# Cross attention and a squared-ReLU MLP: the second layer of the slot-read rows as seven block products, with a split bias and new order keys

## Chip, cores and metric

The kernel runs on one core of one Trainium2 chip. The metric is the device time of that core in microseconds, from the first to the last instruction of one execution. Kernels were timed in turns with the kernel before on the same chip.

## The reference

There are two parts. Eight batches of eight heads (S = 512 rows, Ns = 32 state slots, D = 64) read across from x to the state, and from the state to x. The two results, 512 + 32 rows in each batch, go through one two-layer MLP (512 to 2048 to 512).

```python
scores = scale * x @ state^T;   a  = softmax(scores);    xread = a  @ state   # 512 rows a batch
scores2 = scale * state @ x^T;  a2 = softmax(scores2);   sread = a2 @ x       #  32 rows a batch
rows = concatenate([xread, sread])        # (8 * 544) rows of 8 heads * 64 = 512
h = rows @ w_in                           # 512 -> 2048
g = s * relu(h) ** 2 + b
out = g @ w_out                           # 2048 -> 512, float32
```

The 8 x 32 = 256 rows of `sread` are called the slot-read rows, `sr` in the names of the tiles. They are worked on together, at the end. The constant `b` adds the same vector to every row, `b` times the column sums of `w_out`.

## The kernel before

All work is put into one list of operations. Each has an engine, an estimated duration, a key, what it needs, what it makes and the buffers that it holds. `Plan.order` then simulates the engines and takes, for each engine that is free, the ready operation with the lowest key. The program is written out in that order, so a change of a key or of a duration in the list moves instructions everywhere. These are its lines that the change touches:

```python
class Plan:
    def __init__(self, caps, hop=0.2, look=0.4): ...
    # ... in order():
        def settle(i):
            since[i] = max([ops[i][8]] + [ready[n] for n in ops[i][3]])
    # ...
                    k = ops[i][1] + 20.0 * max(0.0, t)
                    if e == "PE" and ops[i][7] and mode:     # a tiled matmul after a tiled one
                        k -= 4.0
    # ...
                for m in makes:
                    ready[m] = done + self.hop
```

Batches 1 to 7 already compute their second layer as seven block products (in the manner of Strassen and Winograd) in place of eight. The activations are cut into 2 x 2 blocks of rows and hidden columns, `w_out` into 2 x 2 blocks. `pair_sums` makes sums of activation blocks (`pd`), `weight_sum` sums of weight blocks (`u`). The products gather in two PSUM banks `ob`:

```python
    STEPS = [            # bank, activation block, weight block, first, last
        (0, 4, 4, True, False), (1, 6, 6, True, True), (0, 2, 1, False, False), (1, 1, 0, True, False),
        (0, 0, 2, False, False), (1, 3, 7, False, True), (0, 7, 3, False, True),
    ]
    TAKE = {0: ("c11", 0), 2: ("c12", 1), 3: ("c22", 1), 6: ("c21", 0)}     # evict to a new tile, plus bias
    GIVE = {1: "c11", 4: "c22", 5: "c12"}                                   # evict on top of that tile
    PUT = {1: ("c11", 0, 0), 4: ("c22", 1, 1), 5: ("c12", 0, 1), 6: ("c21", 1, 0)}      # store
    # ...
    for b in range(1, B):
        for n in range(7):
            # ... 8 x step_mm (two matmuls 128x256 each), step_out on VectorE, step_put
```

The slot-read rows do it the plain way, in two tiles of 128 rows. The first tile takes 16 matmuls of 512 columns, the second 2 x 16 of 256, so that its first half can be stored early:

```python
    def sr_dst(rr):
        return out_BSn[4 * rr : 4 * rr + 4, S:ST, :]        # 4 batches x 32 rows x 512
    # ...
    for part in range(4):
        add(PEt(0.864), NKF * (B + 1) + part, rows_mm("sr", 0, 4 * part, 4 * part + 4), ...)
    add(DV(0.66), -50, rows_out("sr", 0), ...)
    add(("SP", 0.6), 0, rows_put("sr", 0, sr_dst(0)), ...)                       # 256 KB
    # ... last_mm: the second tile, 256 columns at a time
    for i in range(2):
        for part in range(4):
            add(PEt(0.436), NKF * (B + 1) + 5 + 4 * i + part, last_mm(i, part), ...)
        add(DV(0.4), -50, last_out(i), ...)
        add(("SP", 0.6), 0, last_put(i), ...)                                    # 128 KB each
```

The bias vector is summed over the hidden rows by tiled matmuls, copied, and spread to all partitions by a matmul with a matrix of 1/Ns, in float32:

```python
    def bias_copy(e):
        OSB["wsum"] = opool.tile([P, DM], FP32, name="wsum", tag="osb")
        copy_on(e, OSB["wsum"], OSB["wsum_ps"])

    def bias_spread(e):
        OSB["bias_ps"] = att_ps([P, DM], FP32, "bias_ps")
        mm(OSB["bias_ps"], ones32, OSB["wsum"])
```

The softmax here doesn't subtract the row's maximum and nothing guards it: scores larger than these inputs give would overflow.

## Time and profile before

| kernel before | |
|---|---|
| time | 219.19 us, 218.91 to 219.51 in four runs |
| span of the profiled execution | 217.1 us |
| first matmul of an MLP first layer (`h`) | 13.87 us |
| bias spread | starts at 37.48 us |
| first matmul of the slot-read rows' second layer | 201.87 us |
| last matmul starts | 209.50 us |
| from there to the end ("the tail") | 7.64 us |

The first line of the page gives the busy time of each engine, its share of the span and its instructions. The second is the chain of work that ended last, by engine.

```profile
PE 205.8 (95%) x1967; PEld 132.0 (61%) x1967; DVE 164.6 (76%) x389; ACT 134.5 (62%) x294; POOL 37.4 (17%) x60
...
PE 90%; ACT 2%; DVE 2%; DMA 2%; SPq 0%; issue 0%
```

TensorE (PE) is the limit: it is busy 95% of the span and makes up 90% of the chain. The table by windows shows where that holds. Its columns are the window in us, then busy time and instructions of PE, weight loads (PEld), VectorE (DVE), ScalarE (ACT) and GpSimd (POOL), the granted clock, the mean busy share of the 16 DMA engines (it can read above 1), and GB/s.

```profile
core 0: us, PE busy (x) PEld busy (x) DVE busy (x) ACT busy (x) POOL busy (x), PEclk, DMA share, GB/s
...
50.00:75.00 25.00, 25.00 (x296) 15.71 (x294) 21.66 (x49) 16.60 (x37) 6.28 (x10) 1.00 1.11 149
...
150.00:175.00 25.00, 25.00 (x265) 17.68 (x263) 21.52 (x49) 14.49 (x26) 3.37 (x5) 1.00 0.20 63
...
207.00:208.25 1.25, 1.25 (x14) 1.13 (x12) 0.00 (x0) 0.00 (x0) 0.00 (x0) 1.00 0.63 215
209.75:214.75 5.00, 0.02 (x1) 0.00 (x0) 0.48 (x1) 0.00 (x0) 0.00 (x0) 1.00 0.26 87
```

In mid-kernel PE has no idle time at all, so there only the number and length of its instructions count.

PE's idle time is at the start. Each line of the waits view gives engine and line, what was waited for, total us, number of waits and the longest. Of the tiles, `xn` is x as loaded, `xT` its transpose, `T` the scores, `E` their exponentials, `D` the sums of these, and `M` the state times `w_in`:

```profile
PE xTps L197 <- ACT xn L298: 1.5, 2, 1.2
PE o L197 <- DVE warm L212: 1.2, 1, 1.2
PE h L197 <- ACT g L760: 0.6, 2, 0.4
PE Mps L197 <- DVE M L300: 0.3, 1, 0.3
PE Mps L197 <- ACT M L298: 0.2, 1, 0.2
PE T L197 <- DVE xT L300: 0.2, 1, 0.2
```

The timeline gives start, duration, engine, line, operation and count. Two cuts of it matter, the bias spread and the end:

```profile
37.48 1.02 PE L197 MATMUL bias_ps<-wsum,ones 128*128 128x512 f32 x2
38.34 1.06 PE L197 MATMUL xTps<-ident,xn 128*128 128x128 f16 x16
...
205.11 4.66 PE L197 MATMUL o<-wo,g_sr 128*128 128x512 f16 x36
...
209.81 0.48 DVE L1079 SCALAR_TENSOR_TENSOR osb_last<-o,s_bc,bias_bc 128x256 f32<-128x256 f32 x1 [0.39 <-PE o L197]
...
206.96 0.66 SPq L912 DMA_DIRECT2D out_dram<-osb_sr  x1
209.45 1.41 SPq L1088 DMA_DIRECT2D out_dram<-osb_last  x2
```

Read the starts, not the durations: matmuls overlap, and the next start shows what one took of the stream. The float32 spread is two records and takes 38.34 - 37.48 = 0.86 us. After the last eviction at 209.81 comes only a store. Its issue begins at 210.32 and SyncE (SPq), which waits for all stores before the program may end, is released by it at 216.18, 5.9 us later. The waits of SyncE's queue at the end are these:

```profile
SPq L1134 <- DMA out_dram<-osb_last: 2.6, 2, 1.3
```

### The profile page before, as it was taken

The numbers are of one execution on the slowest core, as the hardware profiler recorded it, in microseconds if no ns is written. First come the engines' busy times: TensorE is split into PE (matmuls) and PEld (weight loads), VectorE is DVE, ScalarE is ACT, GpSimd is POOL, SyncE is SP. The second block draws the span as 40 slices with busy tenths as digits, with TensorE's granted clock in tenths as the row PEclk, the third lists the DMA queues.
The fourth block names the chain that finished last, engine by engine and source line by source line (L and its number), as shares of the span: only waits on it lengthen the run. The fifth ranks groups of instructions, "written<-read, shape, count | busy, mean of one in ns | idle before, by whom it ended". The sixth has DMA issues, their size and how long they took to land.

```text
span 217.1 us, 4922 instructions
## 1 busy us (share of the span) xinstructions
PE 205.8 (95%) x1967; PEld 132.0 (61%) x1967; DVE 164.6 (76%) x389; ACT 134.5 (62%) x294; POOL 37.4 (17%) x60
## 2 busy tenths in 40 slices
PE   5998999999999999999999999999999999999960
PEld 1452334434477776677667666776677777888550
DVE  1268899999888889789978897889888888654320
ACT  4479998587585469747874797479645545332100
POOL 4833100040134251012101210121012102100000
PEclk9999999999999999999999999999999999999997
DMA  6999999999599999413531205122212102111131
GB/s 194 179 199 205 207 202 194 176 147 209 55 161 207 154 194 125 113 51 103 121 76 48 101 32 75 49 73 84 50 48 97 49 8 85 63 48 47 53 85 60
DMA packets 41282, 24.04 MB, mean 111 GB/s; under 512 B 25772, under 2 KB 39340, under 8 KB 41260
## 3 DMA queue, kind: packets, MB, share of 16 engines
q0 software_dynamic: 13840, 15.21, 36.6%
q1 hardware_dynamic: 26860, 8.40, 24.6%
q8 instruction: 15, 0.25, 0.5%
q10 hardware_dynamic: 560, 0.13, 0.3%
q14 instruction: 7, 0.06, 0.1%
HBM read 17.37 MB, written 8.91 MB: 121 GB/s over the span
## 4 chain that ended last, share of the span: by engine, by line
PE 90%; ACT 2%; DVE 2%; DMA 2%; SPq 0%; issue 0%
PE o L197 52%; PE h L197 24%; PE Mps L197 4%; PE h_sr L197 3%; PE D L197 2%; DMA xf<-in_x_dram 2%; ACT g L760 1%; PE V L197 1%; PE xTps L197 1%; PE T L197 1%; DVE g L766 1%; DVE xT L300 1%; PE wsum_ps L197 0%; ACT M L298 0%; PE bias_ps L197 0%; ACT xn L298 0%
## 5 line engine op out<-in xcount | busy, mean ns | idle before, releaser
L760 ACT ACTIVATE g<-h 128x512 f16<-128x512 f32 x125 | 73.3, 604 | 42.8 <-PE h L197 40.9
L197 PE MATMUL h<-a,M 128*128 128x512 f16 x256 | 73.7, 379 | 0.6 <-ACT g L760 0.6
L766 DVE TENSOR_TENSOR g<-g 128x512 f16<-128x512 f16 x128 | 52.9, 420 | 7.0 <-ACT g L760 6.4
L197 PEld LDWEIGHTS <-pd 128*128 128x128 f16 x448 | 43.0, 98 | 19.0 <-issue 2.8
L197 PEld LDWEIGHTS <-g 128*128 128x128 f16 x400 | 38.5, 98 | 22.1 <-issue 1.8
L197 PE MATMUL o<-u,pd 128*128 128x256 f16 x336 | 51.8, 273 | 0.0
L197 PE MATMUL o<-wo,g 128*128 128x256 f16 (+1 forms) x288 | 51.6, 296 | 0.0
L1002 POOL DMA_DIRECT2D out_dram<-c x24 | 16.3, 678 | 104.5 <-DVE c L994 101.5
L298 ACT CAST M<-Mps 128x512 f16<-128x512 f32 x52 | 29.4, 608 | 4.0 <-PE Mps L197 4.0
L197 PEld LDWEIGHTS <-M 128*128 128x128 f16 x256 | 24.2, 98 | 12.5 <-issue 3.9
L994 DVE SCALAR_TENSOR_TENSOR c<-o,s_bc,bias_bc 128x512 f32<-128x512 f32 x28 | 21.0, 751 | 12.7 <-PE o L197 12.7
L197 PE MATMUL o<-u,g 128*128 128x256 f16 x112 | 21.4, 273 | 0.0
L197 PE MATMUL o<-wo,pd 128*128 128x256 f16 x112 | 21.4, 273 | 0.0
L994 DVE SCALAR_TENSOR_TENSOR c<-o,s_bc,c 128x512 f32<-128x512 f32 x21 | 15.8, 750 | 6.7 <-PE o L197 6.6
L778 DVE TENSOR_TENSOR pd<-g 128x1024 f16<-128x1024 f16 x28 | 19.2, 685 | 0.2
L760 ACT ACTIVATE g_sr<-h_sr 128x256 f16<-128x256 f32 x16 | 6.1, 384 | 13.1 <-PE h_sr L197 13.0
L527 ACT ACTIVATE E<-T 128x256 f16<-128x256 f32 x32 | 11.8, 385 | 1.3 <-PE T L197 1.2
L787 DVE TENSOR_TENSOR pd<-g,pd 128x512 f16<-128x512 f16 x28 | 11.7, 419 | 0.0
L789 DVE TENSOR_TENSOR pd<-g,pd 128x512 f16<-128x512 f16 x28 | 11.7, 420 | 0.1
L374 POOL DMA_DIRECT2D xn<-in_x_dram x13 | 10.4, 813 | 7.6 <-DMA wi<-in_moe_w_in_dram 3.2
L546 ACT ACTIVATE D<-D 128x512 f32<-128x512 f32 x16 | 8.7, 582 | 2.5 <-PE D L197 2.4
L197 PE MATMUL h_sr<-srdT,wi 128*128 128x256 f16 x64 | 9.6, 273 | 0.0
(63 smaller groups left out, 157.5 us busy)
## 6 DMA issues: line engine op xcount, KB each, us to landing
out_dram<-c POOLq DMA_DIRECT2D x24, 256.0 KB, 2.5
xn<-in_x_dram POOLq DMA_DIRECT2D x5, 512.0 KB, 22.0
wi<-in_moe_w_in_dram POOLq DMA_DIRECT2D x4, 512.0 KB, 13.5
wo<-in_moe_w_out_dram POOLq DMA_DIRECT2D x4, 512.0 KB, 18.8
xf<-in_x_dram SPq DMA_DIRECT2D x4, 256.0 KB, 3.4
out_dram<-osb POOLq DMA_DIRECT2D x4, 256.0 KB, 5.7
xn<-in_x_dram POOLq DMA_DIRECT2D x8, 128.0 KB, 4.9
out_dram<-c SPq DMA_DIRECT2D x4, 256.0 KB, 2.5
```

What stands on the lines that cost most here:

```text
L197: return nc.tensor.matmul(out, lhsT, rhs, start=start, stop=stop, tile_position=tp, is_transpose=is_transpose, skip_group_check=True,)
L298: nc.scalar.copy(dst, src)
L374: nc.gpsimd.dma_start(out=xn[b][:, h0:h1].rearrange("p h c d -> p h (c d)"), in_=x[b, h0:h1].rearrange("h (q c) d -> q h (c d)", q=P),)
L527: nc.scalar.activation(a["E"][g][:, 256 * m : 256 * m + 256], a["T"][m][:, g, :], AF.Exp, scale=scale, accum_out=a["rs"][:, g, m : m + 1],)
L546: nc.scalar.activation(A[b][f"D{g}"], A[b][f"D{g}"], AF.Ln)
L760: nc.scalar.activation(g_of(name, f), OSB["h", name, f], AF.Relu)
L766: ENG[e].tensor_mul(g_of(name, f), g_of(name, f), g_of(name, f))
L778: nc.vector.tensor_tensor(pd[:, :, 0:2], g4[:, :, 1:2, :].to_broadcast((P, 2, 2, hS)), g4[:, :, 0:4:3, :], ALU.subtract,)
L787: nc.vector.tensor_tensor(pd[:, :, 2], g4[:, :, 3], pd[:, :, 0], ALU.subtract)
L789: nc.vector.tensor_tensor(pd[:, :, 3], g4[:, :, 2], pd[:, :, 2], ALU.subtract)
L994: nc.vector.scalar_tensor_tensor(t, src, s_bc, add, ALU.mult, ALU.add)
L1002: ENG[e].dma_start(dst[:, rows:SCH:2, hD * h : hD * h + hD], SN[b, name])
```

## The change

Three things are changed. The slot-read rows get the same seven products as the batches (seven times eight matmuls of 256 columns in place of 16 of 512 and 32 of 256). These take turns in two PSUM banks of their own, taken from the pool `att` that the attention no longer needs then. VectorE gets 12 pair sums more, 7 evictions in place of 3, and there are four stores of 128 KB. The float32 matmul of the bias becomes two in fp16: the sum rounded to fp16 and the remainder. And the list scheduler is changed: a delay between operations (`hop`) counts only between different engines, a tiled operation that stands alone on TensorE gets a penalty (`solo`), and all keys are set anew, with the estimated landing times of the first loads 0.2 us lower.

```diff
-    def __init__(self, caps, hop=0.2, look=0.4):
+    def __init__(self, caps, hop=0.2, look=0.4, solo=0.0):
...
-            since[i] = max([ops[i][8]] + [ready[n] for n in ops[i][3]])
+            own = set(ops[i][0])
+            since[i] = max(
+                [ops[i][8]]
+                + [ready[n] + (0.0 if own == {made_on.get(n)} else self.hop) for n in ops[i][3]]
+            )
...
+                    if alone and ops[i][7]:
+                        k += self.solo
...
     K = dict(
-        h1=4.3, hs=0.6, M0=-5.6, M1=0.9, T1=0.9, x2=24.4, T2=23.7, D2=25.5, M2=24.1, V0=27.6, V1=20.5, u=12.2,
-        us=5.1, pd1=12.5, o0=9.6, o2=23.0, w=26.2, r=0.7, T=-14.8, D=3.1, Mb=5.5, V=8.6, S=3.6, S0=0.1, E=-4.5,
-        L=-4.6, a4=-4.7, Mc=4.3, pd=3.5, sp=-1.7,
+        h1=4.4, hs=0.6, M0=-5.6, M1=0.9, T1=0.0, x2=24.6, T2=23.7, D2=27.2, M2=35.3, V0=27.7, V1=21.3, u=12.3,
+        us=5.1, pd1=12.5, o0=13.1, o2=23.0, w=26.2, r=0.5, T=-9.8, D=3.1, Mb=6.4, V=8.6, S=3.6, S0=0.1, E=-0.5,
+        L=-6.2, a4=-4.7, Mc=1.5, pd=13.4, solo=2.0, hsr=-4.1, Ssr=0.0,
     )
...
     def bias_copy(e):
-        OSB["wsum"] = opool.tile([P, DM], FP32, name="wsum", tag="osb")
-        copy_on(e, OSB["wsum"], OSB["wsum_ps"])
+        OSB["wsum"] = opool.tile([P, 2, DM], FP16, name="wsum", tag="osb")
+        nc.vector.tensor_copy(OSB["wsum"][:, 0], OSB["wsum_ps"])
+        nc.vector.tensor_tensor(OSB["wsum"][:, 1], OSB["wsum_ps"], OSB["wsum"][:, 0], ALU.subtract)
 
     def bias_spread(e):
         OSB["bias_ps"] = att_ps([P, DM], FP32, "bias_ps")
-        mm(OSB["bias_ps"], ones32, OSB["wsum"])
+        for k in range(2):
+            mm(OSB["bias_ps"], ones_p, OSB["wsum"][:, k], start=(k == 0), stop=(k == 1))
...
+    def bank_of(b, n):
+        if b != "sr":
+            return ob[(STEPS[n][0] + b) % 2]
+        if ("bank", STEPS[n][0]) not in OSB:
+            OSB["bank", STEPS[n][0]] = att_ps([P, DM], FP32, f"osr_{STEPS[n][0]}")
+        return OSB["bank", STEPS[n][0]]
...
             name, rows, h = PUT[n]
+            if b == "sr":
+                dst = out_BSn[4 * rows : 4 * rows + 4, S:ST, hD * h : hD * h + hD]
+                ENG[e].dma_start(dst, SN[b, name][:, 0])
+                return
...
-    for b in range(1, B):
+    for b in [*range(1, B), "sr"]:
+        nb = B if b == "sr" else b
         for n in range(7):
...
-    for part in range(4):
-        add(
-            PEt(0.864), NKF * (B + 1) + part, rows_mm("sr", 0, 4 * part, 4 * part + 4),
...  (the plain second layer of the slot-read rows, last_mm, last_out and last_put go)
```

More of the change, by code (lines that the diff above doesn't have):

```diff
@@ L14 @@
 class Plan:
-    def __init__(self, caps, hop=0.2, look=0.4):
-        self.caps, self.hop, self.look = caps, hop, look
+    def __init__(self, caps, hop=0.2, look=0.4, solo=0.0):
+        self.caps, self.hop, self.look, self.solo = caps, hop, look, solo
         self.ops, self.pool_of, self.users = [], {}, {}
@@ L31, in order @@
         waits, count, cand = {}, {}, {e: set() for e in ("PE", "ACT", "DVE", "POOL", "SP")}
-        since = {}
+        since, made_on = {}, {}
         def settle(i):
-            since[i] = max([ops[i][8]] + [ready[n] for n in ops[i][3]])
+            own = set(ops[i][0])
[3 more added lines that the diff above has]
+            )
             for e in ops[i][0]:
@@ L72, in order @@
                 best = None
+                alone = False
+                if e == "PE" and not mode:
+                    near = [i for i in cand[e] if ops[i][7] and since[i] <= now + 0.3 and soon(i) <= now + 0.3]
+                    alone = len(near) < 2 or sum(len([b for b in ops[i][5] if self.pool_of[b] == "att"]) for i in near[:2]) > (
+                        self.caps["att"] - sum(x not in freed for x in allocs["att"])
+                    )
                 look = self.look if e in ("ACT", "DVE") else 0.06
@@ L123, in order @@
                 for m in makes:
-                    ready[m] = done + self.hop
+                    ready[m], made_on[m] = done, (e if land is None else None)
                 for m in makes:
@@ L240 @@
     nc.vector.memset(ones16, 1.0)
-    ones32 = konst.tile([P, P], FP32, name="ones32")
-    nc.vector.memset(ones32, 1.0 / Ns)
+    ones_p = konst.tile([P, P], FP16, name="ones_p")
+    nc.vector.memset(ones_p, 1.0 / Ns)
     s_bc = konst.tile([P, 1], FP32, name="s_bc")
@@ L306 @@
             "u": 4, "osb": 6, "q": 2, "rs": 3,
-        }
+        },
+        solo=K["solo"],
     )
@@ L389 @@
     nc.gpsimd.tensor_copy(gate, ident16[:, 0:2])
-    seq = [("wi", 0), ("x", 1), ("wi", 1), ("stf1",), ("wo", 0), ("wi", 2), ("wo", 1), ("wi", 3)]
-    seq += [("wo", 2), ("wo", 3), ("x", 2), ("sb",), ("x", 3), ("x", 4), ("x", 5)]
+    SEQ = "wi0 x1 wi1 stf1 wo0 wi2 wo1 wi3 wo2 wo3 x2 sb x3 x4 x5"
+    seq = [(t,) if t in ("stf1", "sb") else (t[:-1], int(t[-1])) for t in SEQ.split()]
     for n, it in enumerate(seq):
@@ L768, in square, with half_of @@
         return fn
+    def half_of(b):
+        return B * Ns // 2 if b == "sr" else S // 2
     def blocks(b, j):
@@ L776, in fn @@
             if n == 0:
-                pd = PD[b, j] = ppool.tile([P, 2, 4, hS], FP16, name=f"pd_{b}_{j}", tag="pd")
+                t = half_of(b)
+                pd = PD[b, j] = ppool.tile([P, 2, 4, t], FP16, name=f"pd_{b}_{j}", tag="pd")
                 nc.vector.tensor_tensor(
                     pd[:, :, 0:2],
-                    g4[:, :, 1:2, :].to_broadcast((P, 2, 2, hS)),
+                    g4[:, :, 1:2, :].to_broadcast((P, 2, 2, t)),
                     g4[:, :, 0:4:3, :],
@@ L878 @@
     add(PEt(0.9), K["w"], bias_sum, [("wo", q) for q in range(4)], ["wsum_ps"], [("att", "wsum_ps")], tiled=True)
-    add(DV(0.6), 20, bias_copy, ["wsum_ps"], ["wsum"], [("att", "wsum_ps"), ("osb", "wsum")])
-    add(PEt(0.88), 24, bias_spread, ["wsum"], ["bias_ps"], [("att", "bias_ps"), ("osb", "wsum")])
+    add(DV(1.25), 20, bias_copy, ["wsum_ps"], ["wsum"], [("att", "wsum_ps"), ("osb", "wsum")])
+    add(PEt(0.44), 24, bias_spread, ["wsum"], ["bias_ps"], [("att", "bias_ps"), ("osb", "wsum")])
     add(DV(0.6), 20, bias_out, ["bias_ps", ("b",)], ["bias"], [("att", "bias_ps")])
@@ L885, in x_dst @@
         return out_BSn[b, 0:S].rearrange("(q c) n -> c q n", c=SCH)[chunk_of(rr)]
-    def sr_dst(rr):
-        return out_BSn[4 * rr : 4 * rr + 4, S:ST, :]
     def rows_mm(name, rr, f0, f1):
@@ L964 @@
     ]
+    def bank_of(b, n):
[4 more added lines that the diff above has]
+        return OSB["bank", STEPS[n][0]]
     def step_mm(b, n, i):
         def fn(e):
-            bank, xa, xw, first, last = STEPS[n]
-            for r in range(2):
+            _, xa, xw, first, last = STEPS[n]
+            for r in range(half_of(b) // P):
                 mm(
-                    ob[(bank + b) % 2][:, hD * r : hD * r + hD],
+                    bank_of(b, n)[:, hD * r : hD * r + hD],
                     row_tile(b, xa, i, r),
@@ L986, in fn @@
         def fn(e):
-            src = ob[(STEPS[n][0] + b) % 2].rearrange("p (r n) -> p r n", r=2)
+            m = half_of(b) // P
+            src = bank_of(b, n)[:, 0 : m * hD].rearrange("p (r n) -> p r n", r=m)
             if n in TAKE:
                 name, h = TAKE[n]
-                t = SN[b, name] = opool.tile([P, 2, hD], FP32, name=f"{name}_{b}", tag="osb")
-                add = bias_bc[:, hD * h : hD * h + hD].unsqueeze(1).to_broadcast((P, 2, hD))
+                t = SN[b, name] = opool.tile([P, m, hD], FP32, name=f"{name}_{b}", tag="osb")
+                add = bias_bc[:, hD * h : hD * h + hD].unsqueeze(1).to_broadcast((P, m, hD))
             else:
@@ L1004, in step_put @@
         return fn
-    for b in range(1, B):
+    nsr = B * Ns
+    for f in range(NKF):
+        hb, gb = ("h", f"hsr_{f}"), ("g", f"gsr_{f // 4}")
+        k = NKF * B + f + K["hsr"]
+        add(
+            PEt(0.436), k, h_mm("sr", f, wi_of(f), lambda: [srdT[:, :, kk, :] for kk in range(NKM)], nsr),
+            [("srT", b) for b in range(B)], [("h", "sr", f)], [hb, gb],
+        )
+        add(AC(0.3), k - 0.5, relu("sr", f, nsr), [("h", "sr", f)], [("r", "sr", f)], [hb, gb])
+        add(DV(0.2), k, square("sr", f), [("r", "sr", f)], [("g", "sr", f)], [gb])
+    for j in range(4):
+        for n in range(3):
+            add(
+                DV(0.335 if n == 0 else 0.2), NKF * B + 4 * j + 4 + K["hsr"] + K["pd"], pair_sums("sr", j, n),
+                [("g", "sr", 4 * j + i) for i in range(4)] if n == 0 else [("pd", "sr", j, n - 1)],
+                [("pd", "sr", j, n)], [("g", f"gsr_{j}"), ("pd", f"pdsr_{j}")],
+            )
+    for b in [*range(1, B), "sr"]:
+        nb = B if b == "sr" else b
         for n in range(7):
             bank, xa, xw, first, last = STEPS[n]
-            bank = (bank + b) % 2
+            own = [("att", f"osr{bank}")] if b == "sr" else []
+            bank = ("sr", bank) if b == "sr" else (bank + nb) % 2
             for i in range(NKF // 2):
@@ L1019 @@
                 else:
-                    needs += bank_free[bank]
+                    needs += bank_free.get(bank, [])
                 add(
-                    PEt(0.218), NKF * (b + 1) + K["S0"] + (n * 8 + i) / K["S"], step_mm(b, n, i), needs,
-                    [("s", b, n, i)], [x for x in bufs if x[0] != "uu"],
+                    PEt(0.218 if b != "sr" else 0.109), NKF * (nb + 1) + K["S0"] + (K["Ssr"] if b == "sr" else 0) + (n * 8 + i) / K["S"], step_mm(b, n, i), needs,
+                    [("s", b, n, i)], [x for x in bufs if x[0] != "uu"] + own,
                 )
@@ L1027 @@
             add(
-                DV(0.66), -50, step_out(b, n), [("s", b, n, NKF // 2 - 1), "bias", ("s",)]
+                DV(0.66 if b != "sr" else 0.4), -50, step_out(b, n), [("s", b, n, NKF // 2 - 1), "bias", ("s",)]
                 + ([("c", b, name)] if n in GIVE else []),
-                [("read", b, n), ("c", b, name)] + ([("done", b, n)]), [out],
+                [("read", b, n), ("c", b, name)] + ([("done", b, n)]), [out] + own,
             )
@@ L1034 @@
                 add(
-                    ("SP", 0.6) if b == B - 1 else ("POOL", 0.7), 0, step_put(b, n),
+                    ("SP", 0.6) if b in (B - 1, "sr") else ("POOL", 0.7), 0, step_put(b, n),
                     [("done", b, n)], [], [out], ("tp", 2.5),
                 )
-    nsr = B * Ns
-    for f in range(NKF):
-        hb, gb = ("h", f"hsr_{f}"), ("g", f"gsr_{f // 4}")
-        k = NKF * B + f
-        add(
-            PEt(0.436), k, h_mm("sr", f, wi_of(f), lambda: [srdT[:, :, kk, :] for kk in range(NKM)], nsr),
-            [("srT", b) for b in range(B)], [("h", "sr", f)], [hb, gb],
-        )
-        add(AC(0.3), k - 0.5, relu("sr", f, nsr), [("h", "sr", f)], [("r", "sr", f)], [hb, gb])
-        add(DV(0.2), k, square("sr", f), [("r", "sr", f)], [("g", "sr", f)], [gb])
@@ L1050 @@
-    for part in range(4):
-        add(
-            PEt(0.864), NKF * (B + 1) + part, rows_mm("sr", 0, 4 * part, 4 * part + 4),
-            [("g", "sr", 4 * part + i) for i in range(4)]
-            + ([("o", "sr", 0, part - 1)] if part else bank_free[0]),
-            [("o", "sr", 0, part)], [("g", f"gsr_{part}")],
-        )
-    add(DV(0.66), -50, rows_out("sr", 0), [("o", "sr", 0, 3)], [("read", "sr", 0)], [("osb", "osr0")])
-    add(("SP", 0.6), 0, rows_put("sr", 0, sr_dst(0)), [("read", "sr", 0)], [], [("osb", "osr0")], ("tp", 2.5))
@@ L1059 @@
-    bank_free[0] = [("read", "sr", 0)]
-    def last_mm(i, part):
-        def fn(e):
-            for f in range(4 * part, 4 * part + 4):
-                mm(
-                    ob[1 - i][:, 0:hD],
-                    g_of("sr", f)[:, P : 2 * P],
-                    wof(f)[:, hD * i : hD * i + hD],
-                    start=(f == 0),
-                    stop=(f == NKF - 1),
-                )
-        return fn
-    def last_out(i):
-        def fn(e):
-            if i == 0:
-                OSB["last"] = opool.tile([P, DM], FP32, name="osb_last", tag="osb")
-            cols = slice(hD * i, hD * i + hD)
-            nc.vector.scalar_tensor_tensor(
-                OSB["last"][:, cols], ob[1 - i][:, 0:hD], s_bc, bias_bc[:, cols], ALU.mult, ALU.add
-            )
-        return fn
@@ L1085, in last_put @@
-    def last_put(i):
-        def fn(e):
-            cols = slice(hD * i, hD * i + hD)
-            nc.sync.dma_start(sr_dst(1)[:, :, cols], OSB["last"][:, cols])
-        return fn
-    for i in range(2):
-        for part in range(4):
-            add(
-                PEt(0.436), NKF * (B + 1) + 5 + 4 * i + part, last_mm(i, part),
-                [("g", "sr", 4 * part + k) for k in range(4)]
-                + ([("ol", i, part - 1)] if part else bank_free[1 - i]),
-                [("ol", i, part)], [("g", f"gsr_{part}")],
-            )
-        add(DV(0.4), -50, last_out(i), [("ol", i, 3)] + ([("lo", 0)] if i else []), [("lo", i)], [("osb", "last")])
-        add(("SP", 0.6), 0, last_put(i), [("lo", i)], [], [("osb", "last")], ("tp", 2.5))
@@ L1106 @@
     landed = {
-        "ident": 3.4, "stf": 5.0, ("xf", 0): 4.0, ("xf", 1): 4.9, ("xf", 2): 6.0, ("xf", 3): 7.0,
+        "ident": 3.2, "stf": 4.8, ("xf", 0): 3.8, ("xf", 1): 4.7, ("xf", 2): 5.8, ("xf", 3): 6.8,
     }
```

## The prediction, made before the changed kernel ran

> **What bounds it now.** TensorE. The page's busy table has matmul at 95% of the 217.1 us span; the chain that ended last is 90% TensorE. In the table by windows it is busy 25.00 of 25 us in every stretch from 50 to 175 us; the waits view gives it 4 us of idle in all, before 29 us. VectorE (76%) and ScalarE (62%) are not limits. After the last matmul (about 209.5 us in the timeline) come a 0.48 us VectorE pass and the last store, some 7 us. So TensorE stream time, the first 30 us and the tail count.
>
> **Stream costs, from the timeline's starts.** A 128x256 matmul takes 0.109 us of stream, a 128x512 0.215. The Trainium skill ("TensorE: Matmul & The Clock Gate", Back-to-back issue gap) gives N/2.4 + 2.5 ns for the warm isolated gap, 109 and 216 ns; the trace agrees. A stretch of tiled matmuls costs about 0.09 us on entry and 0.13 us on leaving above its columns (16 Mps matmuls: 0.65 us between 128-row streams, 0.43 us of columns).
>
> **What the change does.**
> 1. Slot-read second layer: before 16x0.215 + 32x0.109 = 6.93 us, after 7 products x 8 = 56x0.109 = 6.10 us. It is the end of the stream, all on the path: -0.83 us.
> 2. These products, 0.87 us each, alternate on two banks of their own. From the end of the stream into a bank to the end of its 0.48 us VectorE pass the trace shows about 0.83 us, and TensorE starts about 0.05 us after VectorE ends. That just fits: up to 0.1 us of wait at each of five products, I take +0.1 in all.
> 3. Bias: the fp32 spread matmul is two records, 0.86 us of stream; two fp16 of 0.215 replace it: -0.43 us. One more VectorE pass (0.69 us) is hidden.
> 4. Order: 29 tiled stretches instead of 31, one more V-to-Mps switch inside them: -2x0.09 - 0.13 = -0.3 us.
> 5. Start: ScalarE now does the first Ln and Exp before the second E; by the trace's durations the first h matmul moves from 13.9 to about 14.3 us (+0.4). The order after it should remove part of the 1.25 us of waits between 17 and 28 us; I take -0.7. Net -0.3 us, the least certain term.
> 6. VectorE gains 12 pair sums (4x(0.42+0.29+0.29) = 4.0 us), 7 evictions of 0.48 us for 1.7 us before, and the bias part: busy to about 171 us. There is room.
>
> The last store is 128 KB as before, so the tail stays near 7 us.
>
> **Sum.** -0.83 + 0.1 - 0.43 - 0.3 - 0.3 = -1.8 us: **217.5 us**, 8 in 10 between **216.2 and 218.9**. Faster by over 2%: 0.04; within 2%: 0.94; slower: 0.02.
>
> **What would show it.** Last matmul about 1.8 us earlier, tail unchanged; slot-read products in 6.1 to 6.2 us with waits on VectorE below 0.1 us each; the bias spread in 0.43 us; TensorE without idle from 30 us to the end; first h matmul near 14.3 us, smaller waits after it; VectorE near 171 us.
>
> **What would make it wrong.** Batches now fill one bank with a whole product before turning to the other, instead of interleaving two. If VectorE, busier now, has over about 0.6 us queued in front of an eviction, TensorE waits in mid-kernel and the gain is lost. The bank turn-around in the last products may be longer than 0.87 us: 0.2 us at each of five would eat the product saving. The start could be worse than in 5, or weights land later than the new order wants. A gain above 2% needs the start to shrink by over 2 us, which its waits do not offer.

## The result, and the profile after

| | before | after |
|---|---|---|
| time, median (range) | 219.19 us (218.91 to 219.51) | 216.89 us (216.22 to 217.08) |
| span of the profiled execution | 217.14 us | 214.97 us |
| first `h` matmul | 13.87 us | 14.35 us |
| transposes of batch 2 start | 38.34 us | 38.19 us |
| last matmul starts | 209.50 us | 208.39 us |
| tail | 7.64 us | 6.58 us |

The ratio is 0.9889, with a 95% interval of 0.9864 to 0.9915. Ratios are computed as the mean time of one kernel's fast runs over the mean of the other's in the same rounds, so they are not quite the ratio of the medians in the table. The time lies inside the predicted range, 0.6 us below the predicted value. The table already shows that it did not come about as predicted. The transposes of batch 2 start only 0.16 us earlier, where the terms for the start and the bias had promised 0.73, and the tail, which was to stay, is 1.06 us shorter.

The same lines of the page of the kernel after, busy times and chain:

```profile
PE 204.7 (95%) x1976; PEld 132.6 (62%) x1976; DVE 176.0 (82%) x412; ACT 132.5 (62%) x288; POOL 37.3 (17%) x60
...
PE 84%; ACT 5%; DVE 5%; DMA 2%; issue 1%; SPq 0%
```

VectorE rose by 11.4 us, not by the 6.3 us that the prediction had added up. The groups of instructions on the page explain the rest. They give line, engine, operation, shapes and count, then busy us and mean ns:

```profile
L310 ACT CAST M<-Mps 128x512 f16<-128x512 f32 x45 | 25.3, 595 | 7.1 <-PE Mps L209 7.1
...
L312 DVE CAST M<-Mps 128x512 f16<-128x512 f32 x19 | 13.0, 687 | 2.0 <-PE Mps L209 1.9
```

Before, ScalarE had 52 of these 64 casts and VectorE 12. The new order moved seven to VectorE, 7 x 0.687 = 4.8 us. It did no harm, since VectorE was not the limit, but it is a thing that the diff doesn't show and the instruction order does. The table by windows, with the same columns as above:

```profile
50.00:75.00 25.00, 25.00 (x317) 15.54 (x315) 22.68 (x52) 16.34 (x37) 6.02 (x9) 1.00 0.98 140
...
150.00:175.00 25.00, 25.00 (x254) 17.48 (x239) 22.42 (x51) 16.99 (x36) 2.70 (x4) 1.00 0.24 66
...
204.50:205.50 1.00, 1.00 (x12) 0.90 (x10) 0.61 (x2) 0.00 (x0) 0.00 (x0) 1.00 0.77 262
...
208.00:208.40 0.40, 0.40 (x7) 0.35 (x4) 0.32 (x1) 0.00 (x0) 0.00 (x0) 1.00 0.00 0
...
209.00:213.50 4.50, 0.00 (x0) 0.00 (x0) 0.18 (x1) 0.00 (x0) 0.00 (x0) 0.83 0.26 82
```

PE is still without idle in mid-kernel, in spite of the busier VectorE. The third and the last row: 0.77 of the DMA engines and 262 GB/s while a batch's store runs, 0.26 and 82 GB/s while the slot-read stores run alone. The row between them shows that nothing moves from 208.00 to 208.40: the first slot-read store is through before the second begins, so only the last three, 384 KB, follow one another at the end. In the kernel before there is no such break after the last batch store: the share is 0.24 from 208.25 to 209.75 (at only 19 GB/s, for a reason that no run shows) and 0.26 from there to 214.75, so all 512 KB follow one another. PE's waits, and the waits of SyncE's queue at the end:

```profile
PE xTps L209 <- ACT xn L310: 1.3, 2, 1.1
PE o L209 <- DVE warm L224: 1.2, 1, 1.2
PE D L209 <- ACT E L540: 0.7, 1, 0.7
PE h L209 <- ACT g L773: 0.5, 2, 0.3
```

```profile
SPq L1119 <- DMA out_dram<-c_sr: 3.8, 3, 1.5
```

The waits after the first `h` shrank little. The three waits for `xT` and `M` between 17 and 19 us (0.15, 0.21 and 0.25 us in the timeline) are gone, but one of 0.69 us for `E` has come in their place, at 19.56 us. SyncE now waits three times, 1.5 us at the longest, for the slot-read stores. The timeline at the same two places:

```profile
37.75 0.60 PE L209 MATMUL bias_ps<-wsum,ones_p 128*128 128x512 f16 x2
38.19 1.06 PE L209 MATMUL xTps<-ident,xn 128*128 128x128 f16 x16
...
202.39 1.91 PE L209 MATMUL osr<-wo,g_sr 128*128 128x256 f16 x16
204.13 2.78 PE L209 MATMUL osr<-u,pd_sr 128*128 128x256 f16 x24
206.75 1.04 PE L209 MATMUL osr<-wo,pd_sr 128*128 128x256 f16 x8
207.63 1.04 PE L209 MATMUL osr<-u,g_sr 128*128 128x256 f16 x8
...
208.70 0.48 DVE L1018 SCALAR_TENSOR_TENSOR c_sr<-osr,s_bc,bias_bc 128x256 f32<-128x256 f32 x1 [0.39 <-PE osr L209]
...
204.85 4.90 SPq L1027 DMA_DIRECT2D out_dram<-c_sr  x4
```

The bias spread takes 0.43 us of stream (the difference of the rounded starts is 0.44). The 56 product matmuls follow one another without a gap. No PE line carries a wait in brackets, and VectorE sits idle for 0.39 us before each of its evictions from the second on, so the two banks keep up.

From the starts of the matmuls the difference of the spans, -2.17 us, divides into four stretches that follow one another:

| stretch | before | after | difference |
|---|---|---|---|
| start to first `h` | 13.87 | 14.35 | +0.47 |
| first `h` to the transposes of batch 2 | 24.47 | 23.84 | -0.63 |
| from there to the last matmul's start | 171.16 | 170.21 | -0.95 |
| tail | 7.64 | 6.58 | -1.06 |

(The differences are from times to the nanosecond; the last digit can differ from the rounded columns.) Of the -0.63, 0.43 is the bias spread, and 0.20 remain for the waits and the order in this stretch. Of the -0.95, 0.83 is the computed product saving, which leaves -0.12 for the order.

### The profile page after: what moved, and what is told of

Read it like the earlier page. It is cut to its first block, busy times and chain, and to the rows that moved or that the text cites. A ratio compares the mean times of both kernels' runs of the same rounds, so it can differ in the third digit from the quotient of the medians.

```text
span 215.0 us, 4963 instructions
## 1 busy us (share of the span) xinstructions
PE 204.7 (95%) x1976; PEld 132.6 (62%) x1976; DVE 176.0 (82%) x412; ACT 132.5 (62%) x288; POOL 37.3 (17%) x60
## 4 chain that ended last, share of the span: by engine, by line
PE 84%; ACT 5%; DVE 5%; DMA 2%; issue 1%; SPq 0%
PE o L209 47%; PE h L209 22%; PE Mps L209 4%; PE h_sr L209 3%; PE osr L209 3%; ACT g L773 2%; DMA xf<-in_x_dram 2%; DVE g L779 1%; PE D L209 1%; ACT M L310 1%; PE V L209 1%; PE xTps L209 1%; PE T L209 1%; ACT E L540 1%; DVE u L858 1%
## 5 line engine op out<-in xcount | busy, mean ns | idle before, releaser
L209 PEld LDWEIGHTS <-g 128*128 128x128 f16 x400 | 39.0, 98 | 19.6 <-issue 0.6
L209 PE MATMUL o<-u,pd 128*128 128x256 f16 x336 | 45.9, 273 | 0.0
L209 PE MATMUL o<-wo,g 128*128 128x256 f16 (+1 forms) x288 | 45.5, 297 | 0.1
L310 ACT CAST M<-Mps 128x512 f16<-128x512 f32 x45 | 25.3, 595 | 7.1 <-PE Mps L209 7.1
L209 PE MATMUL o<-wo,pd 128*128 128x256 f16 x112 | 16.2, 273 | 0.0
L209 PE MATMUL o<-u,g 128*128 128x256 f16 x112 | 15.5, 273 | 0.0
L312 DVE CAST M<-Mps 128x512 f16<-128x512 f32 x19 | 13.0, 687 | 2.0 <-PE Mps L209 1.9
L773 ACT ACTIVATE g_sr<-h_sr 128x256 f16<-128x256 f32 x16 | 6.1, 383 | 10.5 <-PE h_sr L209 10.4
L559 ACT ACTIVATE D<-D 128x512 f32<-128x512 f32 x16 | 9.6, 601 | 2.0 <-PE D L209 1.9
```

What stands on the lines that cost most here:

```text
L209: return nc.tensor.matmul(out, lhsT, rhs, start=start, stop=stop, tile_position=tp, is_transpose=is_transpose, skip_group_check=True,)
L310: nc.scalar.copy(dst, src)
L312: ENG[e].tensor_copy(dst, src)
L773: nc.scalar.activation(g_of(name, f), OSB["h", name, f], AF.Relu)
```

## The experiments

Two theories compete for the tail. The first: the slot-read stores keep only about four of the 16 DMA engines busy, so their 512 KB form a queue of about 1.5 us for each 128 KB. The queue sets the end, and it is now shorter because its first store is issued 2.1 us earlier (204.85 in place of 206.96) and is half as large. The rival: a store simply takes about that long to land, or the gain is made in the matmul stream and shows in the tail only by chance. The Trainium skill, "DMA: Bandwidth & Descriptors", section "Why a DMA increments its semaphore by 16 and not by 1", says what would make the stores narrow: a transfer is divided by the slowest dimension that is not one of each access pattern, over the largest number up to 16 that divides both. The slot-read store goes to 4 batches x 32 rows x columns, so this gives 4. The trace agrees: a share of 0.26 of 16 engines is 4.2. The prediction had overlooked it.

For the start there are two theories as well. Either ScalarE's new order, which delays the first `h`, costs the kernel that time, or what comes next is bound by loads and the time is lost anyway.

All kernels gave correct results.

### The change once more

No edit.

> The changed kernel itself, beside the others on one chip. Expected as in its first runs: ratio to before about 0.989, span about 215.0 us, last matmul starting about 1.1 us earlier than in before, and the time from the last matmul's start to the end of the span about 1.0 us shorter (6.6 against 7.6 us).

Measured: 216.9 us, ratio 0.9904 (0.9885 to 0.9923); the profile has 6.62 us of tail and first `h` at 14.41. The result repeats. The stretch from the batch-2 transposes to the last matmul was 170.05 us here. With the 0.83 of the products set aside, that is 0.27 below the kernel before, so the order is worth 0.1 to 0.3 us. In the profile of the first run one matmul, at 45.57 us, starts 0.22 us late; here it is 0.07 us late.

### Wide stores, at the price of a strided write: with the change and without

```diff
# a_store16, on the kernel after
-                dst = out_BSn[4 * rows : 4 * rows + 4, S:ST, hD * h : hD * h + hD]
+                j0 = S + Ns // 2 * rows
+                dst = out_BSn[:, j0 : j0 + Ns // 2, hD * h : hD * h + hD].rearrange("b j n -> j b n")
# relu() of the slot-read rows: put them into the order (slot, batch)
+                    dst = dst.rearrange("p (j b) -> p b j", b=B)
+                    src = src.rearrange("p (b j) -> p b j", b=B)
```

The stores now have 16 as their outermost dimension. For that the rows must lie in another order, and the ReLU pass writes them so, with a stride of 16 bytes. `b_store16` does the same to the kernel before.

> The changed kernel with the slot-read tokens ordered slot-major, so that the four stores of the slot-read rows have an outermost size of 16 instead of 4; the instructions of TensorE are the same in the same order. Theory A (these stores run on 4 of the 16 DMA engines, about 1.5 us for 128 KB, and queue behind one another, which sets the end): the last store lands about 2.5 us after its issue begins, as the batch stores do, not 4.9 us; the span ends about 2.3 us sooner, about 212.6 us, ratio to before about 0.979. Rival B (the tail is a fixed landing time and program end): span stays at 215.0 within 0.3 us. Both: stream of TensorE unchanged.

> The kernel before with the same re-ordering of the stores of the slot-read rows and nothing else. Theory A: the last store lands about 2.5 us after its issue begins (5.9 before), span about 213.7 us, ratio to before about 0.984; then the changed kernel with the same stores is faster than this one by about 1.1 us only, the difference of the ends of TensorE, and the other 1.0 us of the measured gain was the store queue. Rival B: span stays near 217.1 us, and the tail's 1.0 us has another cause.

Measured: `a_store16` 216.57 us, ratio 0.9886 (0.9868 to 0.9905); `b_store16` 217.15 us, ratio 0.9916 (0.9898 to 0.9934). The tails fell to 4.02 and 4.08 us, alike in both kernels, and the stores of 128 KB landed 2.3 us after issue, the one of 256 KB 2.9 us. So the stores' narrowness made 3.6 us of the tail before and 2.6 us of the tail after, and the change's own gain in the tail vanishes with it. But the time of the kernel after hardly moved. The view of the tile `g_sr` (count, then min/median/max in ns, first and last start, shape) and PE's waits show why:

```profile
L777 ACT ACTIVATE g_sr<-h_sr x16: 1311/1347/1636, 181.8 to 201.2; 128x256 f16<-128x256 f32 x16
...
PE h_sr L209 <- ACT g_sr L777: 1.1, 2, 0.5
...
PE h L209 <- ACT g_sr L777: 0.5, 1, 0.5
```

The pass took 383 ns before and 1,347 with the strided write. PE waited for it, and the last matmul came 2.3 us later (210.68 in place of 208.39), which ate the tail's 2.56. The experiment proved the tail and hid its value.

### ScalarE's order at the start, by a new plan

```diff
# a_start: the first Exp of the softmax normaliser also waits for the second E
-[("Dl", b, g)]
+[("Dl", b, g)] + ([("E", 0, 1)] if (b, g) == (0, 0) else [])
```

> The changed kernel where the first Exp of the row sums must wait for the second E of batch 0, which restores the order of ScalarE that the kernel before has there (the list schedule places what follows anew). Theory S (the first h matmul moves back from 14.35 to about 13.9 us and all that follows moves with it): span shorter by 0.4 to 0.5 us. Rival (the waits between 17 and 30 us absorb it): the bias matmul and all that follows start within 0.15 us of where they start in the changed kernel, span unchanged within 0.2 us.

Measured: 218.21 us with a wide spread (217.19 to 219.89), ratio 0.9994 (0.9961 to 1.0026). The first `h` came at 13.29 us, and the bias spread 0.5 us earlier than in the kernel after, partly because the clock rose earlier in this profile (see the caution under `a_start_only`). But a new need makes the scheduler reorder everything. The profile, which is of the fastest of the six runs, has waits of 1.0 us on `E` at 17.8 us and of 0.7 us on an output buffer at 46.1 us, and its span is no shorter. The slower runs have no profile. As a test of the start it is inconclusive, and a warning: in a list-scheduled kernel, one dependency more is not one thing changed.

### Wide stores by a strided read

```diff
# a_store16_read: as a_store16, but the permutation is in the read from PSUM
+                    dst = dst.rearrange("p (j b) -> p j b", b=B)
+                    src = src.rearrange("p (b j) -> p j b", b=B)
```

> The changed kernel with slot-major stores as in the run before, but the order is changed where ScalarE reads the PSUM bank (strided read of f32, contiguous write of f16) instead of where it writes. If it was the strided f16 write (16 bytes between elements) that made its pass 1.35 us instead of 0.38 us, the pass is near 0.4 us again, TensorE has no wait on it, the last matmul starts near 208.4 us as in the changed kernel, the last store lands 2.3 us after its issue and the span is near 212.4 us, ratio to before about 0.979. If any strided access of ScalarE costs this, the pass is again above 1 us and the span near 214.7 us.

Measured: 214.03 us, ratio 0.978 (0.9759 to 0.9802). The tail is 4.01 us. The tile view, the DMA view (KB each, us from issue to landing) and the window of the last stores:

```profile
L777 ACT ACTIVATE g_sr<-h_sr x16: 383/383/384, 180.8 to 197.8; 128x256 f16<-128x256 f32 x16
...
out_dram<-c_sr SPq DMA_DIRECT2D x4, 128.0 KB, 2.3
...
208.50:210.00 1.50, 0.00 (x0) 0.00 (x0) 0.00 (x0) 0.00 (x0) 0.00 (x0) 1.00 0.65 171
```

The read with a stride of 128 bytes costs nothing measurable, 383 ns as before. The stores run at a share of 0.65 in place of 0.26 and land in 2.3 us. This kernel has the lowest time. Its ratio says 2.2% faster, but the interval reaches just across 2%, so whether the gain is over 2% stays unclear.

### Wide stores by a strided matmul operand

```diff
# a_store16_moving: as a_store16, the permutation in the moving operand of the first layer
-lambda: [srdT[:, :, kk, :] for kk in range(NKM)]
+lambda: [srdT[:, :, kk, :].rearrange("p b j -> p j b") for kk in range(NKM)]
```

> The same stores, the order changed in the moving operand of the 64 first-layer matmuls of the slot-read rows (256 bytes between its columns). If TensorE reads a strided moving operand at full rate, these matmuls stay at 0.109 us and the span is near 212.4 us, ratio about 0.979; if the stride halves the rate, 64 x 0.109 = 7 us are added to the stream and the kernel is slower than before.

Measured: 236.59 us, ratio 1.0805. The tail is 4.03 us, but the 64 first-layer matmuls of the slot-read rows, whose moving operand has a stride of 256 bytes, became slow (the view begins inside a run of seven of them and shows the last four):

```profile
182.77 1.91 PE L209 MATMUL h_sr<-srdT,wi 128*128 128x256 f16 x4
184.50 0.62 PE L209 MATMUL o<-u,g 128*128 128x256 f16 x4
```

From start to start the four take 184.50 - 182.77 = 1.73 us, 0.432 each in place of 0.109. That is 0.323 x 64 = 20.7 us more, of the 22.6 by which the median lies above that of the version with the strided read. The rest is not placed; this profile also has a granted clock of 0.50 from 194.0 to 200.8 us.

The Trainium skill ("Advanced Engine Details and Errata", section "Memory Cachelines") says that SBUF has 16-byte cachelines and that a different line on each access is penalised. The write with a stride of 16 bytes (x3.5) and the matmul operand with one of 256 (x4.0) agree. It says of PSUM that patterns that are not contiguous slow matmuls, and that every two consecutive elements should be contiguous. ScalarE is not named there, and its strided read of PSUM was free here.

### Wide stores without any permutation

```diff
# a_store_split: four stores of 32 rows each, in turns from two queues
-                ENG[e].dma_start(dst, SN[b, name][:, 0])
+                for q in range(4):
+                    eng = (nc.sync, nc.scalar)[q % 2]
+                    eng.dma_start(dst[q], SN[b, name][32 * q : 32 * q + 32, 0])
```

> The changed kernel with each store of the slot-read rows split into four of 32 rows (outermost size 32), two issued by SyncE and two by ScalarE, no order changed on any compute engine. Theory A (few DMA engines per store): each lands about 2.3 us after issue; the last pair is issued about 0.55 us later than the single store was, so the span is about 1.8 us shorter than the changed kernel's, near 213.1 us, ratio about 0.982. Rival: the landing time is set by something else of these rows (their short runs in memory): span unchanged.

Measured: 214.36 us, ratio 0.9799 (0.9781 to 0.9817), tail 4.28 us. With the batch dimension taken out of each store, the outermost dimension is 32, and the queue is gone. This was a different cure with the same result. Nothing of the layout of `g` was changed, so the cause is the shape of the store and not something that the permutation did besides.

### ScalarE's order at the start, with the rest of the order kept

```diff
# a_start_only: only these steps of the finished order are moved
+    for m, after in ((("R", 0, 0), ("E", 0, 1)), (("a4", 0, 0), ("R", 0, 0))):
+        t = steps.pop(at(m))
+        steps.insert(at(after) + 1, t)
+    # and one dummy matmul each is taken out ahead of D(0,1) and of h(0,0)
```

> The changed kernel with its order kept everywhere but at the start: the first Exp of the row sums goes after the second E on ScalarE, as in the kernel before, and two warm-up matmuls are taken out. Theory S: first h about 0.4 us earlier (near 14.0 us) and span 0.4 us shorter, since the order that follows is the same. Rival: the load of the weights and ScalarE hold the matmuls that follow, the waits between 14 and 28 us grow by what was gained, and the bias matmul starts within 0.15 us of 37.8 us, span unchanged.

Measured: 216.33 us, ratio 0.9888 (0.9867 to 0.9909), no different from the change's own 0.9889 and 0.9904.

```profile
12.82 1.03 PE L209 MATMUL h<-a,M 128*128 128x512 f16 x4
...
14.92 0.62 PE L209 MATMUL xTps<-ident,xn 128*128 128x128 f16 x8 [1.07 <-DMA xn<-in_x_dram]
```

The first `h` is 1.5 us earlier than in the profile of the kernel after, and soon after PE waits 1.07 us for the load of batch 1's x. No gain in time is seen. Why is not settled by this profile. About 0.9 us of the 1.5 is the clock, as the next paragraph shows. And the load varies: it landed at 14.9 us here (4.38 + 10.5), but at 13.6 us in the kernel after (4.29 + 9.3) and at 13.3 us in `a_store16_read`, where no matmul waited for it.

One caution belongs to this. The dummy matmuls at the start are 0.427 us apart until the clock rises and 0.216 after. By the clock records of the traces that switch fell at 7.9 to 9.0 us in some profiles and at 9.7 to 11.0 in others, also of kernels that differ only at the end, and goes with a difference of about 1 us in the first `h`. `a_start_only` is of the early kind and the kernel after of the late one; against `a_store16_read`, which is early and has the start of the kernel after (13.44), its first `h` is only 0.6 us earlier, of which the two dummy matmuls taken out are 0.43. The Trainium skill ("TensorE: Matmul & The Clock Gate", Part 1) calls the window that decides this free-running and variable from run to run. The trace agrees. Comparing stretches from the first `h` on avoids it. Among profiles of one kind the new order is still 0.5 to 0.6 us later (late switch: 13.77 and 13.87 against 14.35 and 14.41; early: 12.85 against 13.44).

### Wide stores in the kernel before

The edit of `a_store16_read`, made to the kernel before.

> The kernel before with slot-major stores of the slot-read rows (order changed in ScalarE's read). Theory A: its tail, from the start of the last matmul to the end of the span, is 4.0 to 4.1 us instead of 7.6, so it is 3.5 us faster than before, ratio about 0.984, and the changed kernel with the same stores (0.978) is ahead of it by only about 1.1 to 1.3 us. If the seven products shorten the tail by something else than the store queue, the tail here stays about 1 us longer than that of the changed kernel with the same stores.

Measured: 215.42 us, ratio 0.9841 (0.9821 to 0.9861), tail 4.09 us. The store shape alone is worth 3.5 us to the kernel before, more than the whole change. With wide stores in both, the change is worth 0.9841 - 0.978 = 0.006, about 1.3 us (the two ratios are from two chips, each against the kernel before on its own). As given it is worth 2.1 to 2.4. The difference of about 1 us is what the change gained only from the narrow store queue.

### The plain second layer put back into the kernel after

```diff
# a_oldsr
-    for j in range(4):           # pair sums of the slot-read rows
-        ...
-    for b in [*range(1, B), "sr"]:
+    for b in range(1, B):
+    ... (rows_mm, last_mm, last_out, last_put and their adds as in the kernel before)
```

> The changed kernel with the second layer of the slot-read rows as in the kernel before (48 matmuls of whole rows, three stores), bias and order keys as changed. Stream: from the transposes of batch 2 to the last matmul 170.2 + 0.83 = 171.0 us. Theory A adds the tail, since the first of the slow stores is 256 KB and comes later: 7.6 us instead of 6.6. In all 1.8 us slower than the changed kernel, ratio about 0.998. If only the stream counts: 0.8 us, ratio about 0.994.

Measured: 218.55 us, ratio 0.9984 (0.9966 to 1.0002), tail 7.56 us, its first slot-read store issued at 206.54. Against the two runs of the change this is 0.8 to 0.95%, or 1.8 to 2.1 us. The saving of the products (0.83) and the tail (7.56 - 6.62 = 0.94) add to 1.77. In the stream of that profile only 0.47 of the 0.83 shows against the first profile of the change, which held the odd wait of 0.22 us, and 0.62 against the second. The rest of it is not placed; it may be the order that the scheduler made new.

### The float32 bias put back

```diff
# a_bias32: bias_copy and bias_spread as before; the durations in the list stay as after, so the order does too
+        mm(OSB["bias_ps"], ones32, OSB["wsum"])
```

> The changed kernel with the f32 bias matmul put back and the same order of instructions. The bias spread takes 0.86 us of stream instead of 0.43; since TensorE never waits after it but for 0.2 us, all of it should arrive at the end: from the first h matmul to the transposes of batch 2 24.27 us instead of 23.84, time about 0.43 us longer, ratio about 0.992.

Measured: 217.43 us, ratio 0.9925 (0.9904 to 0.9945). From first `h` to the transposes of batch 2 the profile has 24.36 us in place of 23.84, and the spread takes 0.86 us again. The trace shows the 0.43 us. The times are in the right direction, but the intervals overlap with those of the change, so the times alone don't prove it.

### The old schedule with the new products and the new bias

```diff
# a_oldkeys: class Plan, K and the landing times as before (hsr and Ssr set to 0, no solo)
```

> Seven products and the f16 bias with the list schedule and the keys of the kernel before. If the new order is worth only its tiled stretches (29 here become 33): about 4 x 0.22 = 0.9 us of stream more than the changed kernel, less what its start gains by the old order (up to 0.4 us): ratio about 0.992. If the old keys also leave VectorE late at the banks, now that it has more work, TensorE waits in mid-kernel and the ratio is near 1.

Measured: 220.18 us (218.58 to 221.28), ratio 1.0052 (1.0016 to 1.0087). The products and the bias under the old keys are slower than the kernel before. PE waits for a transfer in mid-kernel, and in the products it waits for VectorE:

```profile
PE V L197 <- DMA aT<-a: 1.6, 1, 1.6
...
206.38 2.17 PE L197 MATMUL osr<-u,pd_sr 128*128 128x256 f16 x16 [0.47 <-DVE c_sr L1005]
...
211.02 1.03 PE L197 MATMUL osr<-u,g_sr 128*128 128x256 f16 x8 [0.25 <-DVE c_sr L1005]
```

The two-bank turn-around, which cost nothing in the change, costs here: evictions of VectorE come too late for it, by 1.0 us in three waits. There are also 33 tiled stretches on PE in place of 29. The new rules and keys of the scheduler, which were only tested together, are thus part of the product change and not an addition that could be left out. The old keys had not been tuned for this list of operations, so the run says nothing of old against new keys in general.

## Why the prediction was right, and where it was not

The total was predicted as -1.8 us and came out as -2.2 in the span, within the range. Two of its terms were wrong, and their errors have opposite signs: the start gave 0.57 us less than predicted and the tail 1.06 us more. That the total came so near is in part luck.

- **What bounds the kernel: right.** PE is without idle in mid-kernel before and after.
- **Products, -0.83: right.** 56 starts 0.109 us apart fill 6.11 us. The Trainium skill ("TensorE: Matmul & The Clock Gate", section "Back-to-back issue gap") gives 109 ns for 256 columns by its formula, and the trace has 0.109.
- **Turn-around of the banks, +0.1: nothing.** No PE wait in the products. `a_oldkeys`, with 1.0 us of such waits, shows that the danger was real and that the new rules and keys together took it away.
- **Bias, -0.43: right.** 0.86 to 0.43 us of stream, shown by the trace of the change and undone by `a_bias32`.
- **Order, -0.3: about right.** -0.1 to -0.3 in two profiles. The trace shows a tiled stretch to cost about 0.09 us on entry and 0.12 to 0.13 on leaving, and there are 29 in place of 31. The Trainium skill ("TensorEngine Tiling (Array Packing)", section "Key Properties") says that a change of tiling mode drains the engine; the trace agrees in that there is extra time at each change, and gives it a size.
- **Start, "Net -0.3 us, the least certain term": wrong.** The delay of the first `h` came as predicted (+0.47). But the stretch after it, the bias aside, shrank by 0.2 us and not by 0.7, so the net is +0.27. Three small waits gave way to one of 0.69 us for `E`. Whether the earlier order of ScalarE would have kept 0.5 us of it is not shown: `a_start_only` brought no time, but its profile met a late load of batch 1's x.
- **Tail: wrong. This is the step that failed: "The last store is 128 KB as before, so the tail stays near 7 us."** The tail fell by 1.06 us, about half of the gain. The size of the last store does not set the tail. The backlog of the stores ahead of it does, since all of them go through about four DMA engines: 512 KB in one stretch before, the last 384 KB after, once the first store is through. `a_store16`, `b_store16`, `a_store16_read`, `a_store_split` and `b_store16_read` show it: with wide stores all tails are 4.0 to 4.3 us, before and after the change. `a_oldsr` brings 7.56 us back.
- **VectorE at 171 us: 176.0**, because seven casts moved to it. No harm, as said.
- **"A gain above 2% needs the start to shrink by over 2 us": wrong as a reason.** The change itself was indeed well within 2%. But `a_store16_read`, at 2.2% with an interval of 0.9759 to 0.9802, and `a_store_split` come to that border without touching the start. The room was in the tail, which had been taken for fixed.

What stays open: the 0.2 to 0.4 us of the product saving that the stream of `a_oldsr` does not show. And a start better than either order was not found: `a_start` was confounded, and in the profile of `a_start_only` a wait for a load took the gain, so what bounds the start is open.

## What to carry to other kernels

When stores stand at the end, look at the DMA share while they run alone: 0.26 of 16 engines was a queue on four of them, and a reordered or split destination (outermost dimension 16 or 32 here) was worth more than the whole arithmetic saving. Choose where a permutation is paid by measuring it: the same one cost nothing in ScalarE's read of PSUM, about 2.3 us in its write, and over 20 us in a matmul operand. A sum that comes out right is no proof of its terms, so divide the measured span into the same terms as the prediction and compare each.

## What the Trainium skill lacked or had wrong

- "DMA: Bandwidth & Descriptors", section "Why a DMA increments its semaphore by 16 and not by 1": its rule for the number of engines holds here, and the page's "Rules for kernel authors" warns of an outermost dimension below 16, but it gives no measured rate for a store on few engines. Measured with an outermost dimension of 4: a share of 0.26, 82 to 87 GB/s, about 1.4 to 1.6 us for each 128 KB in a queue; with 16, 2.3 us from issue to landing and no queue. It doesn't say what several such stores in a row cost by queueing behind one another. The last narrow store landed 5.9 us after issue in the kernel before and 4.9 us in the kernel after, a wide one 2.3 us.
- "Advanced Engine Details and Errata", section "Memory Cachelines": it gives no times. Measured: ScalarE writing fp16 128x256 with a stride of 16 bytes, 1,347 ns against 383; a matmul whose moving fp16 operand has a stride of 256 bytes, 0.432 us of stream against 0.109; ScalarE reading float32 from PSUM with a stride of 128 bytes, 383 against 383. ScalarE's reads of PSUM are not named there.
- "TensorE: Matmul & The Clock Gate", section "Back-to-back issue gap": it gives 131 ns as the sustained rate for 512 columns in a stream of weight loads and matmuls. The streams here took 215 ns, the section's figure for an isolated one.
- "TensorEngine Tiling (Array Packing)", section "Key Properties": no size is given for the drain at a change of mode; about 0.09 us on entry and 0.12 to 0.13 us on leaving here.
